# Local attention and a gated product on one core: scores in four 64x64 tiles, and another order of the stays

## The chip, the core and the metric

The kernel runs on one core of a Trainium2 chip. The metric is device time of one execution in microseconds (us). Three runs of the kernel before gave 747.78 us in the median (745.87 to 752.30).

The engines that matter here: TensorE (PE in the profile) multiplies; its weight loads are listed apart (PEld). VectorE (DVE) and ScalarE (ACT) do the element-wise work, SyncE (SP) issues the transfers. GpSimd (POOL) is all but unused.

## The reference

```python
def _attn_ref(q, k, v, n_global, n_local):      # 4 batches, 8 heads, 768 tokens, 64 wide
    scores = (1 / np.sqrt(D)) * np.matmul(q, k.transpose(0, 1, 3, 2))
    rel = pos[:, None] - pos[None, :]
    is_global = pos[None, :] < n_global           # 8
    is_local = (rel >= 0) & (rel < n_local)       # 96
    ...                                           # bias -slope[head] * distance
    scores = np.where(is_global | is_local, scores + bias, -1e9)
    a = softmax(scores)
    return np.matmul(a, v)

def _moe_ref(x, w_a, w_b, w_out):               # 3072 x 512, 512 x 1536, 1536 x 512
    a = x @ w_a
    b = x @ w_b
    return a * b @ w_out
```

A token sees at most 96 tokens behind it and the first 8 of its sequence. The attention's output, 3072 tokens by 512, is x of the gated product. Weights come as 64-bit floats and are turned into 32-bit ones on the chip.

## The kernel before, in words

**Units and chunk pairs.** The 3072 tokens are six units of 512. The hidden width of 1536 is twelve chunks of 128, taken two at a time as six chunk pairs. Each unit has to meet each chunk pair once: 36 meetings. A *stay* is a stretch in which the weights of a few chunk pairs stay on the core; a *pass* is one unit within a stay. Before, a stay has two chunk pairs. ORDER (line 48) lists pairs 0 and 1 with units 0, 1, 2; pairs 2 and 3 with units 2, 1, 0; pairs 4 and 5 with all six; pairs 2 and 3 with units 5, 4, 3; pairs 0 and 1 with units 3, 4, 5. Where a unit leaves its accumulators and comes back, its partial sums are written out and read again (evict, line 1020).

**A meeting.** Values are split into a high and a low part (split, line 397: a cast and a subtraction), and a product takes three matmuls, high by high, high by low, low by high. In a *plain* meeting (project_plain, line 892) four groups of twelve matmuls, 512 tokens wide, make al and ga for two chunks; VectorE multiplies them (h), and cut (line 919) splits h into hh and hl. In a *Winograd* meeting (project, line 930) seven groups of twelve matmuls, 256 wide, do the same work, with more element-wise work: sums of weight pieces, of token pieces (forms, line 776) and of results. Before, the six meetings of the first stay are plain and thirty are Winograd. Both end with back (line 993), 24 matmuls of 512 columns into four accumulators acc.

**Weights.** to32 (line 329) loads a piece of 512 KB as words (wr) and makes 32-bit floats of it with two ACT and four DVE instructions. Six pieces make a chunk pair. In the first stay the pieces are split at once into the tiles w (convert_plain); for later use, convert makes the Winograd sums and writes them to DRAM (dw), and load_w reads them back and splits them. Chunk pairs 0 and 1 are thus converted twice, 48 pieces in all.

**Attention.** A granule is one unit by one pair of heads: 24 granules, four blocks of 128 tokens each. For a block (line 561), two matmuls of 128 by 128 by 168 columns make the scores of 64 tokens of both heads each: q is laid out with zeros so that one head's 64 channels meet its own keys alone, and rows of the result are 64 tokens of head 0, then of head 1. These go to one bank, ps. DVE adds the mask and takes the minimum (line 579), ACT makes exp and the sum (line 595), DVE or ACT normalizes. For unit 0 the probabilities are turned on TensorE (direct, line 695, tile pt); for the others on DVE and through DRAM (turn, carry; tiles tt, mir, px, py). values (line 662) multiplies with v, in tiles of 64 columns, two side by side, one for each head, into pa. Units 0, 1, 2 leave their result on the core in X; units 3, 4, 5 go to DRAM (dx) and are loaded back. Splitting X gives xp (plain) or xf (Winograd).

**Order.** Every operation is put on a list with a due time, its reads and writes, and the cost that the planner assumes (Schedule, line 134). order() runs a clock of its own over it and gives every engine its operations in a fixed sequence; where ACT or DVE can do a copy, it picks one. Tables of numbers (START, SPANS, CONV, ...) set the due times: SPANS is the stretch of passes in which a unit's attention is done, CONV that in which a chunk pair is converted. On the chip each engine keeps its sequence and waits where an input is late.

## Time and profile before

| what | us |
|---|---|
| median of three runs | 747.78 |
| profiled execution, device time | 750.77 |
| its span, first to last instruction | 748.9 |
| PE busy | 705.6 |
| PEld busy | 632.9 |
| DVE busy | 580.1 |
| ACT busy | 390.3 |
| end of the first pass (last back of unit 0 with pair 1) | 112.5 |
| end of the first stay | 231 |
| last matmul ends | 743.15 |

The page of the profile gives busy time by engine, then the span in 40 equal slices with a digit of tenths for each engine, the clock that TensorE was granted and what the transfers moved. Groups of instructions are listed by line with their mean duration and the idle time ahead of them. Timeline rows give start and duration of single instructions or runs of them. A row's duration holds a tail in which the next instruction is already running, so what an instruction occupies is read from start to start. A matmul of two 32-bit operands shows as two records; the counts in the timeline are records.

### The profile page before, as it was taken

How to read it: one execution, taken by the hardware profiler on the slowest of the kernel's cores; microseconds unless marked ns; L12 is line 12 of the kernel's file. 1: busy time of each engine (PE TensorE's matmuls, PEld its weight loads, DVE VectorE, ACT ScalarE, POOL GpSimd, SP SyncE). 2: the span in 40 equal slices, each digit the busy share in tenths (PEclk: the TensorE clock that was granted, in tenths of full speed). 3: DMA queues.
4: the chain of work that ended last, by engine and by line, in shares of the span. 5: the costliest groups of instructions: out<-in, count | busy, mean ns of one | idle time of the engine just before them, and what ended most of it. 6: DMA issues, size and time to landing. Idle time of an engine off the chain costs nothing.

```text
span 748.9 us, 13720 instructions
## 1 busy us (share of the span) xinstructions
PE 705.6 (94%) x4888; PEld 632.9 (85%) x4888; DVE 580.1 (77%) x1601; ACT 390.3 (52%) x980; POOL 1.8 (0%) x8
## 2 busy tenths in 40 slices
PE   4889798998989999999999999999999999999996
PEld 4767677776789889989999888999999999999995
DVE  5899989787789879988999798957467475676643
ACT  2897577456547676557665554633434332342310
POOL 0000000000000000000000000000000000000000
PEclk8999899998999999999999999999999999999999
DMA  7578898999988989998879798542423234232411
GB/s 287 195 245 274 277 301 300 286 331 285 289 323 255 322 305 314 325 320 287 281 268 317 245 288 252 207 155 85 141 71 103 81 113 133 92 112 101 127 71 60
DMA packets 71868, 165.25 MB, mean 221 GB/s; under 512 B 8304, under 2 KB 26864, under 8 KB 70000
## 3 DMA queue, kind: packets, MB, share of 16 engines
q1 hardware_dynamic: 71792, 164.30, 65.8%
q8 instruction: 40, 0.66, 0.4%
q14 instruction: 36, 0.29, 0.1%
HBM read 113.41 MB, written 50.86 MB: 219 GB/s over the span
## 4 chain that ended last, share of the span: by engine, by line
PE 50%; DVE 21%; DMA 19%; ACT 6%; issue 2%; SPq 1%; DVEq 0%; ACTq 0%
PE acc L1003 16%; PE al L861 15%; PE ga L861 11%; DMA wr<-wts 9%; PE ps L564 3%; DVE tt L654 2%; DMA qk<-qk 2%; PE pa L668 2%; DVE t L579 2%; DMA py<-mir 2%; ACT t L595 2%; DVE wm L389 2%; DVE wm L372 2%; DMA wl_A<-dw_A 2%; PE ga L880 1%
## 5 line engine op out<-in xcount | busy, mean ns | idle before, releaser
L1003 PE MATMUL acc<-w_O,hh 128*128 128x512 f32 x576 | 196.4, 400 | 0.7 <-DVE w_O L320 0.7
L1003 PEld LDWEIGHTS acc<-w_O,hh 128*128 128x128 f32 x576 | 108.3, 188 | 23.8 <-DVE w_O L320 1.5
L1003 PE MATMUL acc<-w_O,hl 128*128 128x512 f32 x288 | 113.5, 394 | 0.0
L595 ACT ACTIVATE t<-t,sm 128x168 f32<-128x168 f32 x192 | 81.9, 428 | 39.4 <-DVE sm L579 39.0
L861 PE MATMUL al<-xf_T,w_S 128*128 128x256 f32 x720 | 97.5, 285 | 3.8 <-ACT s L310 3.8
L564 PE MATMUL ps<-qk 128*128 128x168 f32 x384 | 79.2, 338 | 20.6 <-DVE sm L579 13.7
L861 PEld LDWEIGHTS al<-xf_T,w_S 128*128 128x128 f32 x720 | 91.7, 190 | 5.8 <-ACT s L310 4.4
L564 PEld LDWEIGHTS ps<-qk 128*128 128x128 f32 x384 | 63.7, 207 | 31.0 <-DVE sm L579 19.5
L310 ACT COPY s<-al 128x512 f32<-128x512 f32 x70 | 40.9, 584 | 83.6 <-PE al L861 77.7
L579 DVE CUSTOM_DVE_ANT_0 t<-ps,mask 128x168 f32<-128x168 f32 x192 | 56.5, 323 | 17.9 <-PE ps L564 17.7
L310 ACT CAST hh<-h 128x512 fp32r<-128x512 f32 x62 | 38.2, 618 | 58.1 <-DVE h L320 33.5
L1003 PEld LDWEIGHTS acc<-w_O,hl 128*128 128x128 f32 x288 | 54.2, 188 | 9.5
L945 DVE TENSOR_TENSOR s<-ga,s 128x512 f32<-128x512 f32 x60 | 41.0, 683 | 21.9 <-PE ga L861 21.2
L320 DVE TENSOR_TENSOR hl<-h,hh 128x512 fp32r<-128x512 f32 x72 | 48.6, 683 | 8.9 <-ACT hh L310 8.6
L861 PE MATMUL ga<-xf_T,w_S 128*128 128x256 f32 x360 | 49.2, 286 | 1.2 <-DVE s L945 1.2
L861 PEld LDWEIGHTS al<-xf_B,w_A 128*128 128x128 f32 x360 | 46.7, 189 | 2.5 <-issue 0.3
L861 PE MATMUL al<-xf_B,w_A 128*128 128x256 f32 x360 | 48.5, 284 | 0.0
L861 PE MATMUL al<-xf_T,w_A 128*128 128x256 f32 x360 | 48.3, 284 | 0.0
L861 PE MATMUL ga<-xf_B,w_A 128*128 128x256 f32 x360 | 48.2, 284 | 0.0
L861 PE MATMUL ga<-xf_B,w_S 128*128 128x256 f32 x360 | 48.2, 283 | 0.0
L861 PEld LDWEIGHTS ga<-xf_T,w_S 128*128 128x128 f32 x360 | 45.8, 190 | 1.9 <-DVE s L945 1.6
L654 DVE STREAM_TRANSPOSE tt<-t 128x256 f32<-128x256 f32 (+1 forms) x160 | 45.9, 344 | 0.7 <-ACT t L632 0.5
(99 smaller groups left out, 1179.6 us busy)
## 6 DMA issues: line engine op xcount, KB each, us to landing
wr<-wts SPq DMA_DIRECT2D x48, 512.0 KB, 4.6
qk<-qk SPq DMA_DIRECT2D x24, 976.0 KB, 8.8
mir<-tt SPq DMA_DIRECT2D x20, 768.0 KB, 4.1
vt<-vd SPq DMA_DIRECT2D x24, 512.0 KB, 5.7
X<-dx SPq DMA_DIRECT2D x11, 1024.0 KB
part<-o SPq DMA_DIRECT2D x32, 256.0 KB, 3.6
px<-mir SPq DMA_DIRECT2D x60, 128.0 KB, 3.8
wl_S<-dw_S SPq DMA_DIRECT2D x28, 256.0 KB, 3.0
```

Source lines behind the costliest of these rows:

```text
L310: self.nc.scalar.copy(out(), src())
L320: lambda e: self.nc.vector.tensor_tensor(out(), a(), b(), op=op),
L372: lambda e: nc.vector.scalar_tensor_tensor(mi(), high(), -0x40000000, mi(), op0=ALU.bitwise_and, op1=ALU.bitwise_or),
L389: lambda e: nc.vector.tensor_tensor(mi(), mi(), low(), op=ALU.add),
L564: nc.tensor.matmul(ps[:, s * KW : s * KW + KW], qk[:, (2 * i + s) * P : (2 * i + s) * P + P], qk[:, k0 : k0 + KW], start=True, stop=True, ...
L579: lambda e, i=i, w=w, ps=ps, j=j, kind=kind: nc.vector.tensor_tensor_reduce(t[:, i, w], ps[:, w], self.mask[p][:, kind, w], -0.125, 3.0e38 ...
L595: lambda e, i=i, w=w, j=j: nc.scalar.activation(t[:, i, w], t[:, i, w], AF.Exp, bias=sm[:, 0, j : j + 1], scale=-1.0, accum_out=sm[:, 1, j ...
L654: nc.vector.transpose(dst[:, s, b, e0 : e0 + n], src)
L668: nc.tensor.matmul(pa[64 * h : 64 * h + 64, i * P : i * P + P], vt[:lanes, v0 : v0 + 64], k[:, 2 * h : 2 * h + 2, :, i].rearrange("p g s k ...
L861: self.nc.tensor.matmul(bank[:, ab * HT : ab * HT + HT], w[:, a, (2 * ab + c) * P : (2 * ab + c) * P + P], x[:, b, c], start=first, stop=F ...
L945: lambda e: nc.vector.tensor_tensor(s[:, :], bank[:, :], s[:, :], op=ALU.add),
L1003: self.nc.tensor.matmul(acc[i][:, :], a[:, rows], w[:, b], start=first and f == 0 and k == 0, stop=False, skip_group_check=True,)
```

## The change

**Scores.** For two blocks at a time, q is laid out without zeros, and each head's scores are matmuls of 64 rows by 64 columns: head h reads partitions 64h to 64h+63, the two halves of 64 tokens go to columns 0 to 63 and 64 to 127, and the heads write to two different banks. A half of tokens takes 168 columns in one matmul or in two (104 and 64): six matmuls a block and twelve for two blocks, where there were two a block. q with keys shrinks from 1952 to 1440 columns, the masks' table from 1344 to 672, and a result row is a token, so a mask tile is made head by head (eight mask instructions instead of four, half as wide). The table is loaded ahead of the first q and keys.

**Stays.** The first stay has chunk pairs 0, 1, 2, all plain, and units 0 to 3: twelve plain meetings, 24 Winograd. Then stays of pairs 3 and 4 (units 3, 2, 1, 0), pair 5 (0, 1, 2, 3), pairs 5 and 2 (4, 5), 3 and 4 (5, 4), 0 and 1 (4, 5): 18 passes instead of 15. A pair that stays is not loaded again. Pairs 0, 1 and 2 are converted twice now, 54 pieces. Unit 3 leaves its result on the core too. For units 1, 2, 3 the value product of a granule is put on the list after the scores of the next.

**Unit 0 in halves.** Its first two granules hold tokens 0 to 255 of all eight heads, the other two tokens 256 to 511 (entry). Its split, its products and its cut are done by halves of 256 tokens, the first half's before the second half's attention is done. Due times of the start are tables of their own now.

```diff
@@ constants @@
-ORDER = ((0, (0, 1, 2)), (1, (2, 1, 0)), (2, (0, 1, 2, 3, 4, 5)), (1, (5, 4, 3)), (0, (3, 4, 5)))
-PASSES = [(g, u) for g, us in ORDER for u in us]
-SPANS = {1: (0.0, 0.5), 2: (0.5, 1.5), 3: (2.5, 5.0), 4: (5.0, 7.5), 5: (7.5, 10.0)}
-NEAR = (0, 1, 2)
-STD = tuple((0, u) for u in NEAR)
+STAYS = (
+    ((0, 1, 2), (0, 1, 2, 3), True),
+    ((3, 4), (3, 2, 1, 0), False),
+    ((5,), (0, 1, 2, 3), False),
+    ((5, 2), (4, 5), False),
+    ((3, 4), (5, 4), False),
+    ((0, 1), (4, 5), False),
+)
+PASSES = [(k, u) for k, stay in enumerate(STAYS) for u in stay[1]]
+SPANS = {1: (0.0, 0.6), 2: (0.85, 1.6), 3: (1.6, 2.6), 4: (3, 7), 5: (6.79, 11.5)}
+NEAR = (0, 1, 2, 3)
...
-START = 44000.0
+START = 25980.0
...
+HALF0 = 24080.0
+HALF1 = 35730.0
...
+def entry(u, g, i):
+    if u:
+        return g, i
+    return 2 * (g % 2) + i // 2, 2 * (g // 2) + i % 2
@@ granule_ops @@
+        for r in range(2):
             self.count += 1
-            tag = "psS" if u else FIRST["psS"][self.count % len(FIRST["psS"])]
-            ps = self.bank(tag, f"ps{n}_{i}")
-
-            def scores(e, i=i, ps=ps):
-                for s in range(2):
-                    k0 = QN + i * KB + 64 * s
-                    nc.tensor.matmul(
-                        ps[:, s * KW : s * KW + KW],
-                        qk[:, (2 * i + s) * P : (2 * i + s) * P + P],
-                        qk[:, k0 : k0 + KW],
-                        start=True,
-                        stop=True,
-                        skip_group_check=True,
+            tags = self.early_bank("psS", u, p, self.count)
+            ps = [self.bank(tags[h], f"ps{n}_{r}_{h}") for h in range(2)]
+
+            def scores(e, r=r, ps=ps):
+                for b in range(2):
+                    i = 2 * r + b
+                    q0, k0, c0 = i * P, QN + i * KB, b * KW
+                    for s, c, k, w in ((1, 0, 64, KW), (0, 0, 64, KX), (0, KX, 0, 64)):
+                        for h in range(2):
+                            rows = slice(64 * h, 64 * h + 64)
+                            nc.tensor.matmul(
+                                ps[h][64 * s : 64 * s + 64, c0 + c : c0 + c + w],
+                                qk[rows, q0 + 64 * s : q0 + 64 * s + 64],
+                                qk[rows, k0 + k : k0 + k + w],
+                                start=True,
+                                stop=True,
+                                skip_group_check=True,
+                                tile_position=(64 * h, 64 * s),
+                            )
+
+            op(due, scores, [qk], ps, pe=720)
-            op(due, scores, [qk], [ps], pe=580)
...
+        if before:
+            before()
...
-            op(due, turn, ts, [(tt, half)], dve=2 * dve(256) + 2 * dve(128))
+            op(due, turn, ts, [(tt, half)], dve=dve(512) + dve(256))
...
@@ values: unit 0 alone @@
+            a, h = 2 * (p % 2), p // 2
+            self.copy(
+                due + VLAG,
+                lambda: x[:, a : a + 2, HT * h : HT * h + HT],
+                lambda: pa[:, :].rearrange("p (a b) -> p a b", a=2),
+                T,
+                [pa],
+                [(x, (a, h)), (x, (a + 1, h))],
+                psum=True,
+            )
...
@@ attention @@
+        late = None
         for p in range(NPAIR):
+            then = self.granule_ops(u, p, dues[p], x, d, late)
+            if u in LAGGED:
+                late = then
+            else:
+                then()
+        if late:
+            late()
...
@@ plain_forms @@
+        for hs, at in ((((0,), due[0]), ((1,), due[1])) if u == 0 else (((0, 1), due),)):
+            c = slice(HT * hs[0], HT * hs[-1] + HT)
+            n = HT * len(hs)
+            for p in range(NPAIR):
+                f = done[p]
...
@@ project_plain @@
+        for hs, at in ((((0,), due[0]), ((1,), due[1])) if i == 0 else (((0, 1), due),)):
+            c = slice(HT * hs[0], HT * hs[-1] + HT)
+            w = HT * len(hs)
+            st = 12 * pe(w)
+            for f in range(2):
+                ws = [self.w[fp, PLAIN[2 * f + k]] for k in range(2)]
+                al, ga = self.bank("al", f"al{n}_{f}{hs}"), self.bank("ga", f"ga{n}_{f}{hs}")
+                s = self.sbuf([P, T], F32, "s", f"s{n}_{f}{hs}", 3)
+                h = hb[f]
+                t = at + 2 * f * st
+                self.plain_product(t, al, ws, 0, x, hs)
+                self.copy(
+                    t + st,
+                    lambda s=s, c=c: s[:, c],
+                    lambda al=al, c=c: al[:, c],
+                    w,
+                    [al],
+                    [s],
+                    psum=True,
+                )
+                self.plain_product(t + st, ga, ws, 1, x, hs)
...
@@ run @@
-        x0 = self.attention(0, 0.0, START - ATT0)
-        self.convert_plain(0, START - CONV0, STEP0)
+        x0 = self.attention(0, STEPS0)
+        self.convert_plain(0, QUADS0)
+        xf = {0: self.plain_forms(0, (HALF0 - FORM0, HALF1 - FORM0), x0)}
+        self.convert_plain(1, QUADS1)
+        self.convert_plain(2, QUADS2)
-        xf = {0: self.plain_forms(0, START - FORM0, x0)}
-        self.convert_plain(1, START + CONV1, 2500.0)
...
-            if i and PASSES[i - 1][0] != s:
-                for fp in (2 * s, 2 * s + 1):
-                    self.load_w(fp, t - 0.9 * fpt + (fp % 2) * fpt, 0.09 * fpt)
+            if i and PASSES[i - 1][0] != stay:
+                for k, fp in enumerate(fps):
+                    if fp not in STAYS[stay - 1][0]:
+                        self.load_w(fp, t - 0.9 * fpt + k * fpt, 0.09 * fpt)
...
+                if not i:
+                    due = [h + k * GAP for h in (HALF0, HALF1)]
...
+                if not i:
+                    prev([d + 48 * pe(HT) for d in due])
+                    prev = None
...
@@ build @@
-        width = 8 * KW
-        nc.sync.dma_start(tiles["qk0"], a["qk"][0, 0])
+        width = 4 * KW
         nc.sync.dma_start(
             tiles["X"].rearrange("p a b -> p (a b)")[:, :width], a["pos"][:, :width]
         )
         nc.sync.dma_start(tiles["slope"], a["pos"][:, width:])
+        nc.sync.dma_start(tiles["qk0"], a["qk"][0, 0])
```

What this does to the sequences is shown at two places. First TensorE, around the first product of unit 0; ps is a bank of scores, pa a value product, al and ga the products with chunk pair 0, w0_ its weights. Before:

```order
L564 MATMUL ps1_0_3_578<-qk0_78 128x168 x2
L880 MATMUL al0_0_0_593<-xp0_0_313,w0_A11_0_499 128x512 x3
L880 MATMUL al0_0_0_593<-xp0_1_448,w0_A11_0_499 128x512 x3
L880 MATMUL al0_0_0_593<-xp0_2_565,w0_A12_0_539 128x512 x3
L880 MATMUL al0_0_0_593<-xp0_3_581,w0_A12_0_539 128x512 x3
L880 MATMUL ga0_0_0_620<-xp0_0_313,w0_A11_0_499 128x512 x3
L880 MATMUL ga0_0_0_620<-xp0_1_448,w0_A11_0_499 128x512 x3
```

After, in unit 0's last granule (ps0_3; L581 is the score line, L943 the product line; the product of the first chunk stands 28 rows further up):

```order
L581 MATMUL ps0_3_1_0_574<-qk1_79 64x168
L581 MATMUL ps0_3_1_1_576<-qk1_79 64x168
L581 MATMUL ps0_3_1_0_574<-qk1_79 64x104
L581 MATMUL ps0_3_1_1_576<-qk1_79 64x104
L581 MATMUL ps0_3_1_0_574<-qk1_79 64x64
L581 MATMUL ps0_3_1_1_576<-qk1_79 64x64
L943 MATMUL al0_0_1(0,)_591<-xp0_0_361,w0_A21_0_423 128x256 x3
L943 MATMUL al0_0_1(0,)_591<-xp0_1_372,w0_A21_0_423 128x256 x3
L943 MATMUL al0_0_1(0,)_591<-xp0_2_458,w0_A22_0_456 128x256 x3
L943 MATMUL al0_0_1(0,)_591<-xp0_3_482,w0_A22_0_456 128x256 x3
```

Before, the first product stands behind all four granules of unit 0, and a product row is 512 wide. Now products of the first half, 256 wide, stand among the scores of unit 0's last granule (ps0_3), and a block's scores are six rows in two banks.

Second VectorE, where unit 1's token tiles xp1 are made, which the second pass waits for; wm is a weight piece on its way, hl the low half of a product. Before:

```order
L389 ISA wm1_5_1061<-wr1_5_1012,wm1_5_1061 128x1024
L579 ISA t2_0_1140,sm2_0_1141<-ps2_0_0_1127,mask1_135 128x168
L579 ISA sm2_0_1141 128x1
L579 ISA t2_0_1140,sm2_0_1141<-ps2_0_0_1127,mask1_135 128x168
L579 ISA sm2_0_1141 128x1
L909 TENSOR_TENSOR h0_1_1_1149<-ga0_1_1_1065,s0_1_1_1063 128x512
L320 TENSOR_TENSOR w1_O1_0_1143<-wm1_5_1061,w1_O1_0_1143 128x512
L320 TENSOR_TENSOR xp1_0_1110<-X_81,xp1_0_1110 128x512
```

After:

```order
L988 TENSOR_TENSOR h0_2_0_1432<-ga0_2_0(1,)_1569,s0_2_0(1,)_1519 128x256
L342 TENSOR_TENSOR w2_O1_0_1592<-wm2_5_1510,w2_O1_0_1592 128x512
L342 TENSOR_TENSOR hl0_2_0_1459<-h0_2_0_1432,hh0_2_0_1450 128x256
L988 TENSOR_TENSOR h0_2_1_1564<-ga0_2_1(1,)_1602,s0_2_1(1,)_1558 128x256
L334 CAST xp1_1_1628<-X_81 128x512
L334 CAST hh0_2_1_1567<-h0_2_1_1564 128x256
L376 TENSOR_SCALAR wm3_0_1619<-wm3_0_1619 128x512
L342 TENSOR_TENSOR hl0_2_1_1590<-h0_2_1_1564,hh0_2_1_1567 128x256
L342 TENSOR_TENSOR xp1_0_1626<-X_81,xp1_0_1626 128x512
L342 TENSOR_TENSOR xp1_1_1628<-X_81,xp1_1_1628 128x512
```

Before, xp1 stands behind the last piece of chunk pair 1 (w1_O1); now behind the last piece of chunk pair 2 (w2_O1), and behind the third meeting of unit 0 (h0_2, hl0_2). VectorE's instructions up to the last hl of the first pass are 359 before and 390 now.

490 lines of the change are left out of this document (255 added, 235 removed).

## The prediction

> **What bounds the kernel now.** I read the page first, then stretches of the span, then the waits, then the cadence of single matmuls.
>
> The page: span, busy time, and in 40 slices PE's busy tenths and the transfers' GB/s.
>
> ```profile
> span 748.9 us, 13720 instructions
> PE 705.6 (94%) x4888; PEld 632.9 (85%) x4888; DVE 580.1 (77%) x1601; ACT 390.3 (52%) x980; POOL 1.8 (0%) x8
> PE   4889798998989999999999999999999999999996
> GB/s 287 195 245 274 277 301 300 286 331 285 289 323 255 322 305 314 325 320 287 281 268 317 245 288 252 207 155 85 141 71 103 81 113 133 92 112 101 127 71 60
> ```
>
> PE is busy 94%, and what it misses lies in the first third. The same in stretches that end where passes end (busy us of PE, PEld, DVE, ACT, POOL; then clock, transfer share, GB/s):
>
> ```profile
> 0.00:50.00 50.00, 33.02 (x272) 29.10 (x273) 36.98 (x170) 33.21 (x123) 1.75 (x8) 0.93 0.66 234
> 50.00:112.50 62.50, 56.25 (x306) 44.21 (x305) 57.75 (x205) 44.65 (x129) 0.00 (x0) 0.92 0.89 287
> 112.50:231.00 118.50, 109.18 (x648) 91.19 (x648) 95.98 (x298) 69.66 (x179) 0.00 (x0) 0.94 0.89 297
> 231.00:309.00 78.00, 76.55 (x578) 70.18 (x578) 70.75 (x202) 52.82 (x133) 0.00 (x0) 1.00 0.92 307
> 309.00:468.00 159.00, 155.49 (x1189) 142.82 (x1188) 141.31 (x397) 90.19 (x236) 0.00 (x0) 1.00 0.86 286
> 468.00:743.20 275.20, 275.15 (x1905) 255.39 (x1903) 176.61 (x336) 99.81 (x187) 0.00 (x0) 1.00 0.33 109
> ```
>
> From 468 us on PE never stops. Between 50 and 112.5 DVE is busy 57.75 of 62.50; from 50 to 309 the transfers are at 0.89 to 0.92. PE's waits by releaser (total, times, longest) put DVE first:
>
> ```profile
> PE ps L564 <- DVE sm L579: 13.7, 11, 4.0
> ```
>
> Now what PE's work takes at its best pace: three pieces of the chain, then single records, where a step is read from start to start.
>
> ```profile
> 143.87 2.79 PE ga L880 x12
> 606.86 5.60 PE acc L1003 x24
> 612.46 1.44 PE al L861 x12
> ```
>
> ```profile
> 20.20 0.27 PE L707 MATMUL pt<-ident,t 128*64 128x128 f32 x1
> 20.31 0.27 PE L704 MATMUL pt<-ident,t 128*104 128x128 f32 x1
> ...
> 24.11 0.44 PE L668 MATMUL pa<-px,vt 104*64 104x128 f32 x4
> 24.39 0.39 PE L668 MATMUL pa<-py,vt 128*64 128x128 f32 x4
> 24.61 0.39 PE L668 MATMUL pa<-px,vt 104*64 104x128 f32 x4
> ...
> 25.71 0.39 PE L668 MATMUL pa<-py,vt 128*64 128x128 f32 x4
> 26.03 0.32 PE L704 MATMUL pt<-ident,t 128*104 128x128 f32 x1
> ...
> 65.04 0.84 PE L564 MATMUL ps<-qk 128*128 128x168 f32 x4
> 65.60 0.51 PE L1003 MATMUL acc<-w_O,hh 128*128 128x512 f32 x1
> ...
> 112.14 0.40 PE L1003 MATMUL acc<-w_O,hh 128*128 128x512 f32 x1
> ...
> 742.75 0.40 PE L1003 MATMUL acc<-w_O,hh 128*128 128x512 f32 x1
> ```
>
> A Winograd meeting is 7 x 1.44 + 5.60 = 15.68, a plain one 4 x 2.79 + 5.60 = 16.76. A block's scores take 0.56 (65.04 to 65.60), so one matmul of 168 columns 0.28. A value product takes 1.92 (24.11 to 26.03), a turn 0.11. Before: 30 x 15.68 + 6 x 16.76 + 96 x 0.56 + 24 x 1.92 + 64 x 0.11 = 470.4 + 100.6 + 53.8 + 46.1 + 7.0 = 677.9. The last matmul ends at 743.15, so 65.3 us are lost to idle time and a low clock. Counting PE's sequence up to the ends of passes in the same way gives 74.2 of work by 112.5 (36 blocks, 7 value products, 64 turns, 96 matmuls of plain products, 48 of back; 38 lost), 174.0 by 231 (57 lost), 249.2 by 309 (60 lost), 402.1 by 468 (66 lost), and nothing after. So the time is PE's work, plus what the start loses while DVE and the transfers cannot feed PE, plus 5.75 behind the last matmul.
>
> **PE's work after the change.** Plain meetings: six more, 6 x (16.76 - 15.68) = +6.5. Unit 0's three meetings in halves: 288 matmuls at 1.44/12 = 0.120 instead of 144 at 2.79/12 = 0.2325, +1.1. Turns and value products keep their counts.
>
> Scores: two blocks were four matmuls, 1.12. Now they are twelve, and each of the four 64x64 tiles streams 168 columns for each block. If all four tiles run side by side, two blocks stream 2 x 0.28 = 0.56. To this comes the change of tile shape. The value product shows it: its groups step by 0.22, but the first takes 0.28 and the way out, 25.71 to 26.03, takes 0.32; in and out 0.16. I take 0.72 for two blocks: 48 x (0.72 - 1.12) = -19.2. The value rows also show that two column tiles do run side by side: four records, two matmuls of 128 columns, step by 0.22, and one matmul of 168 columns takes 0.28, so 128 of them would take 0.21 alone. Two row tiles at once no row shows. From above: at the value product's step of 55 ns a record, 24 records and the 0.16 make 1.48, dearer than now by 0.36, or 17 us in all. From below: if the switches hide under neighbours, 0.56, 8 us better than my figure.
>
> The Trainium skill speaks against this edit in one place: "TensorEngine Tiling (Array Packing)", Key Properties, says that a change of tiling mode drains TensorE. By that rule 48 more score groups pay a drain each; the trace agrees, with the 0.16 in and out of the value product, and without it the sum would be 48 x 0.16 = 7.7 us lower.
>
> Sum: 677.9 - 19.2 + 6.5 + 1.1 = 666.3.
>
> **What the start loses.** VectorE sets the end of the first pass, since unit 1 needs it and so does the last cut. Its costs:
>
> ```profile
> L320 DVE TENSOR_TENSOR h<-s 128x256 f32<-128x256 f32 x90 | 37.2, 418 | 1.1
> L389 DVE CUSTOM_DVE_ANT_0 wm<-wr,wm 128x1024 uint16<-128x1024 uint16 x48 | 32.8, 683 | 1.2 <-ACT wr L382 0.5
> L372 DVE SCALAR_TENSOR_TENSOR wm<-wr,wm 128x512 int32<-128x512 int32 x48 | 32.8, 683 | 0.3
> L362 DVE TENSOR_SCALAR wm<-wm 128x512 int32<-128x512 int32 x48 | 20.0, 418 | 0.4
> L320 DVE TENSOR_TENSOR w_A<-wm,w_A 128x512 fp32r<-128x512 f32 x10 | 6.8, 681 | 0.1
> ```
>
> The six pieces of chunk pair 2 come into the first pass: each 2 x 0.418 + 2 x 0.683 + 0.681 = 2.88, together 17.3. The products and low halves of unit 0 are 24 of 256 (0.418) where they were 8 of 512 (0.683): +4.6. Four score tiles fewer and fewer, wider turns and copies give back some 3. That is 19 us of durations in 31 more instructions (359 to 390); each duration holds a tail under the next one, as here 0.57 against a step of 0.48:
>
> ```profile
> 8.47 0.57 DVE L495 TENSOR_SCALAR X<-X,nf 128x672 f32<-128x672 f32 x1 [3.72 <-DMA X<-pos]
> 8.95 0.56 DVE L496 TENSOR_SCALAR X<-X,nf 128x672 f32<-128x672 f32 x1
> ```
>
> So +16 of occupied time. Against it: these rows wait 3.72 for the table, which now goes first and is half as long; I take 3 off. The first pass then ends at 112.5 + 16 - 3 = 125.5, if DVE stays as full as it was (94.7 busy of 112.5). PE's work up to there, counted from the new sequence, is 83.4: 32 blocks, 7 value products, 64 turns, 288 half-wide matmuls, 72 of back. Loss 42, against 38. Ends: if half of DVE's 17.8 us of idle time goes, because PE's products start early and hand it work, the loss is 33; if DVE is only as full as from 112.5 to 231 (0.81), its 111 us end at 137 and the loss is 54.
>
> Passes 2 to 4 have three meetings each, so PE has 196 us of work there. The transfers listed up to there, added up by tile size, are some 54 MB, 275 GB/s. From 112.5 to 231 before, 297 GB/s ran beside 100 us of PE work, that is, transfers held PE back; it lost 18.5. I charge 6.
>
> Over the whole program transfers fall a little:
>
> ```profile
> wr<-wts SPq DMA_DIRECT2D x48, 512.0 KB, 4.6
> qk<-qk SPq DMA_DIRECT2D x24, 976.0 KB, 8.8
> wl_S<-dw_S SPq DMA_DIRECT2D x28, 256.0 KB, 3.0
> ```
>
> q with keys: 24 x (976 - 720) KB less, six raw pieces and six weight loads more, one unit load less: 3 MB less in all. But passes 9 to 12 (pair 5 alone) have 71 us of PE work, and 25 MB are listed in them: 350 GB/s, where the best slice above has 331. Charged for passes 5 to 12: 8; before, 309 to 468 lost 6.5. For the rest, no loss, as now.
>
> **Sum.** 666.3 + 42 + 6 + 8 = 722.3, with 5.75 a span of 728. The profiled execution took 750.77 for a span of 748.9, so 730; it lay 3 above the median of the runs. I predict 727 us. With the ends above: best, 0.56 a score group and 33 lost at first, 710; worst within this account, 54 lost at first and ten more in passes 9 to 12, 749.
>
> **Rivals.**
>
> *The row tiles take turns.* If the two heads' tiles cannot stream together, the sequence, which puts the heads next to each other, leaves nothing side by side: a block streams 2 x (168 + 104 + 64) columns, at 0.28 for 168 that is 1.12, two blocks with the switch 2.40. 48 x (2.40 - 0.72) = +81, some 15 of it under DVE's time at the start: 793. It decides from 1.2 a group on. For it: no row shows two row tiles. Against it: two column tiles do overlap, and each head has its own bank. The Trainium skill, "TensorE: Matmul & The Clock Gate", Measured speedup vs the span model, measured row and column tiles together, 10.6 times for sixteen; by that rule this rival falls, but no row here can show it. 7%.
>
> *Issue paces the small matmuls.* Twelve small matmuls with their loads replace four; at 1.1 to 1.48 a group (the bound from above) it is 745 to 763. Against it: the value product's 55 ns is two overlapped matmuls of 0.21 each in four records, which its columns explain without issue. 11%.
>
> *VectorE stretches the first pass.* Chunk pair 2's pieces stand ahead of xp1 on DVE, so a late piece holds unit 1 and all PE behind it; the loss is 54 and not 42: 739. For it: DVE 0.92 busy from 50 to 112.5. 8%.
>
> *The short stay runs dry.* 25 MB at 300 GB/s are 83 us for 71 of work, some 10 more than charged: 737. For it: shares near 0.9 up to 468 us. 12%.
>
> *The halves fill the start.* Loss of 30 or less in the first pass and little behind it: under 714. For it: PE idles or runs slow for 38 of 112.5, and most of unit 0's work no longer waits for its last granule. 17%.
>
> My own case, 714 to 738, has 45%.
>
> **Chances.** A difference of over 1% (under 740.3, over 755.3) is about what a measurement tells from none. Faster: 45 + 17, 10 of the short stay's 12, 4 of the first pass's 8, 1 of issue's 11: 0.77. Within 1%: 2 + 4 + 6 = 0.12. Slower: 4 + 7 = 0.11. The range 704 to 750 leaves out the row tiles' 7, the upper part of the issue case (6) and some 5 below.
>
> **What would show it.** Score groups of two blocks that step by about 0.72 from start to start, heads' records starting a few tens of ns apart; 2.4 would be the first rival, 1.1 to 1.5 the second. The first unit-0 product before 35 us, the first pass ending near 125; 137 and later would be the third rival. PE's idle time in the passes of pair 5 near 5; over 12 would be the short stay. From about 480 us on, PE without a gap. I am wrong at the root if the score groups cost less and the end doesn't follow: then PE's work was not what the first 300 us wait for.

## The result, and the profile after

Over four runs of each the changed kernel takes 725.02 us in the median (720.99 to 728.68) and the kernel before 748.65 us (745.87 to 752.30); the ratio is 0.968, with a 95% interval of 0.9613 to 0.9748. The forecast was 727. The profiled execution of the changed kernel is the slowest of its four, 728.68 us for a span of 726.4; the profile of before had 750.77 and 748.9. So it is 22.5 us of span that have to be found.

The page of the changed kernel: span, busy time by engine, PE's busy tenths and GB/s in 40 slices.

```profile
span 726.4 us, 15134 instructions
PE 693.5 (95%) x5584; PEld 605.8 (83%) x5584; DVE 578.9 (80%) x1544; ACT 387.7 (53%) x989; POOL 1.8 (0%) x8
PE   5698998999999999999999999999999999999996
GB/s 296 213 163 259 269 294 300 267 305 250 304 280 303 253 335 247 262 266 228 221 249 232 294 259 301 245 201 230 233 337 151 146 59 102 131 145 102 74 73 62
```

Stretches of the changed kernel that end where passes end (length; busy time of PE, PEld, DVE, ACT, POOL; then clock, transfer share, GB/s). The second row ends with the first pass, the third with the second, the fifth with the first stay, the seventh with pair 5's passes.

```profile
0.00:50.00 50.00, 33.49 (x397) 28.75 (x398) 44.43 (x185) 38.57 (x130) 1.83 (x8) 0.90 0.65 233
50.00:118.70 68.70, 64.44 (x638) 56.39 (x638) 63.67 (x211) 50.16 (x144) 0.00 (x0) 0.98 0.83 261
118.70:208.50 89.80, 85.94 (x714) 66.98 (x714) 67.28 (x231) 50.59 (x150) 0.00 (x0) 0.98 0.84 284
208.50:272.80 64.30, 64.30 (x489) 50.83 (x488) 50.67 (x142) 41.67 (x117) 0.00 (x0) 1.00 0.92 301
272.80:328.60 55.80, 55.72 (x367) 46.14 (x366) 42.81 (x97) 29.31 (x65) 0.00 (x0) 1.00 0.75 257
328.60:473.40 144.80, 143.23 (x1235) 129.56 (x1233) 130.57 (x333) 80.65 (x199) 0.00 (x0) 1.00 0.77 255
473.40:545.60 72.20, 71.85 (x570) 65.80 (x569) 68.48 (x150) 37.32 (x84) 0.00 (x0) 1.00 0.73 247
545.60:720.10 174.50, 174.50 (x1188) 161.35 (x1186) 110.25 (x202) 59.46 (x105) 0.00 (x0) 1.00 0.33 103
```

Subtract PE's busy time from the length of each row: PE idles 26.6 us in these eight rows, and 37.6 in the six rows of before. Multiply each length by what its clock lacks of 1.00: before, 50 x 0.07 + 62.5 x 0.08 + 118.5 x 0.06 = 15.6 us; now 50 x 0.10 + 68.7 x 0.02 + 89.8 x 0.02 = 8.2. That is an upper bound of what a slow clock cost, since PE idles for part of those stretches. So of the 22.5 us, 10.9 are idle time, up to 7.4 are clock, and the remaining 4 or so are PE's own work and the tail behind the last matmul (5.75 before, 6.3 now).

PE's waits of the changed kernel by releaser (total, times, longest): the wait for DVE that came first before, 13.7 us, has shrunk to 1.9.

```profile
PE ps L581 <- DMA qk<-qk: 7.0, 1, 7.0
PE pt L749 <- DVE t L661: 4.2, 2, 3.5
...
PE ps L581 <- DVE sm L602: 1.9, 3, 1.3
```

Single records of PE in the changed kernel: start, duration, shape, records. First the first product of unit 0, then two score groups between plain products of unit 1.

```profile
35.22 2.86 PE L943 MATMUL al_0(0,)_510<-xp,w_A 128*128 128x256 f32 x12
...
128.53 0.82 PE L581 MATMUL ps<-qk 64*64 64x168 f32 x24
129.28 3.05 PE L943 MATMUL ga_0(0, 1)_1772<-xp,w_A 128*128 128x512 f32 x12
132.26 0.82 PE L581 MATMUL ps<-qk 64*64 64x168 f32 x24
133.00 3.06 PE L943 MATMUL al_1(0, 1)_1823<-xp,w_A 128*128 128x512 f32 x12
136.00 0.82 PE L581 MATMUL ps<-qk 64*64 64x168 f32 x24
```

The first product starts at 35.22 where it started at 50.01. A score group steps by 0.75 (128.53 to 129.28). But a product between two groups steps by 2.98 (129.28 to 132.26), where a product alone takes 2.79: a whole turn, group and product, takes 3.72 to 3.74, so a group costs 0.94 and not 0.72. In this trace a product with a group on one side only takes 2.89, so each edge of a group costs its neighbour about 0.1. Over the 36 groups that stand without a wait between products or back's matmuls, a group with both edges costs 0.94 in the median (0.91 to 1.05).

With the prediction's own paces (a group at 0.72), PE's sequence up to the ends of passes gives this account. What a group costs beyond 0.72 stands under "lost" here, and so does time at a low clock:

| up to the end of | ends at | PE's work | lost | lost by the forecast |
|---|---|---|---|---|
| the first pass | 118.7 | 83.4 | 35.3 | 42 |
| the fourth pass | 328.6 | 279.8 | 48.8 | 48 |
| pair 5's passes | 545.6 | 491.0 | 54.6 | 56 |
| the last matmul | 720.1 | 666.2 | 53.9 | 56 |

### The profile page after: what moved, and what is told of

Same layout as the page of the kernel before. It is cut to its first block, busy times and chain, and to the rows that moved or that the text cites. A ratio compares the mean times of both kernels' runs of the same rounds, so it can differ in the third digit from the quotient of the medians.

```text
span 726.4 us, 15134 instructions
## 1 busy us (share of the span) xinstructions
PE 693.5 (95%) x5584; PEld 605.8 (83%) x5584; DVE 578.9 (80%) x1544; ACT 387.7 (53%) x989; POOL 1.8 (0%) x8
## 4 chain that ended last, share of the span: by engine, by line
PE 68%; DMA 12%; DVE 11%; ACT 5%; issue 2%; SPq 1%; DVEq 0%; ACTq 0%
PE acc L1099 19%; PE al L922 16%; PE ga L922 12%; DMA wr<-wts 8%; PE ps L581 4%; PE pa L701 3%; ACT t L619 1%; DMA py<-mir 1%; DVE tt L677 1%; DMA X<-dx 1%; DVE t L602 1%; DVE wm L394 1%; ACT wm L369 1%; DVE wm L411 1%; SPq L323 1%
## 5 line engine op out<-in xcount | busy, mean ns | idle before, releaser
L922 PE MATMUL al<-xf_T,w_S 128*128 128x256 f32 x576 | 76.8, 283 | 0.0
L922 PEld LDWEIGHTS al<-xf_T,w_S 128*128 128x128 f32 x576 | 72.2, 189 | 0.5
L332 ACT CAST hh<-h 128x512 fp32r<-128x512 f32 (+1 forms) x62 | 36.6, 592 | 50.2 <-DVE h L342 22.5
L1099 PEld LDWEIGHTS acc<-w_O,hl 128*128 128x128 f32 x288 | 54.3, 188 | 10.5 <-DVE hl L342 1.1
L581 PEld LDWEIGHTS ps<-qk 64*64 64x64 f32 x1152 | 36.3, 142 | 28.1 <-issue 14.2
L581 PE MATMUL ps<-qk 64*64 64x168 f32 (+2 forms) x1152 | 43.6, 278 | 14.4 <-DMA qk<-qk 7.0
L369 ACT ACTIVATE wm<-wr 128x512 f32<-128x512 f32 x54 | 36.2, 670 | 34.7 <-DMA wr<-wts 25.2
L342 DVE TENSOR_TENSOR hl<-h,hh 128x512 fp32r<-128x512 f32 (+1 forms) x78 | 49.8, 642 | 5.2 <-ACT hh L332 4.9
L677 DVE STREAM_TRANSPOSE tt<-t 128x512 f32<-128x512 f32 x80 | 41.1, 552 | 0.8 <-ACT t L658 0.4
L404 ACT ACTIVATE wr<-wr 128x512 int32<-128x512 uint32 x54 | 36.2, 673 | 7.2 <-DMA wr<-wts 4.3
L701 PE MATMUL pa<-px,vt 104*64 104x128 f32 x384 | 38.9, 278 | 1.2 <-DMA px<-mir 1.2
L701 PE MATMUL pa<-py,vt 128*64 128x128 f32 x384 | 38.0, 273 | 1.1 <-DMA py<-mir 1.0
```

The lines of the kernel that those rows point to most:

```text
L332: self.nc.scalar.copy(out(), src())
L342: lambda e: self.nc.vector.tensor_tensor(out(), a(), b(), op=op),
L369: lambda e: nc.scalar.activation(m(), high().bitcast(F32), AF.Abs),
L404: lambda e: nc.scalar.activation(low(), low().bitcast(U32), AF.Copy, scale=2.0**-29),
L581: nc.tensor.matmul(ps[h][64 * s : 64 * s + 64, c0 + c : c0 + c + w], qk[rows, q0 + 64 * s : q0 + 64 * s + 64], qk[rows, k0 + k : k0 + k + ...
L677: nc.vector.transpose(dst[:, :, e0 : e0 + n], src[:, :, c0 : c0 + 32 * n].rearrange("p j (e k) -> p j e k", e=n),)
```

## The experiments

Each starts from the changed kernel. "First pass" ends are those of its profiled execution.

### What a score group costs

**Each group twice.** All matmuls of a group are issued a second time into the same place.

```diff
-                for b in range(2):
+                for b in (0, 1, 0, 1):
                     i = 2 * r + b
```

> The new kernel with each group's twelve score matmuls issued twice into the same places (the same result). Theory (PE's work is what the end waits for): 0.56 more a group without another change of tile shape, 48 x 0.56 = 27, of which some 5 hide at the start: 745 to 752. Rival (up to 300 us the scores hide behind VectorE and the transfers): 36 of 48 groups lie there, 7 to 12 more, 732 to 737.

Measured: 751.88 us (748.30 to 756.84), ratio to the kernel before 1.0064 [1.0029, 1.0098], so 27 us over the changed kernel. Its timeline, two groups of twice the records:

```profile
128.79 3.04 PE L943 MATMUL al_0(0, 1)_1930<-xp,w_A 128*128 128x512 f32 x12
131.76 1.41 PE L581 MATMUL ps<-qk 64*64 64x168 f32 x48
133.10 3.06 PE L943 MATMUL ga_0(0, 1)_1988<-xp,w_A 128*128 128x512 f32 x12
```

The group steps by 1.34 in place of 0.75, so 24 records, the work alone, take 0.59 (48 x 0.59 = 28 us, and 27 were measured). By the forecast's 0.28 for 168 columns, two tiles at a time would take 1.12 for them and four at once 0.56: four tiles do run side by side. The product beside the group takes 2.97 as before. So of a group's 0.94, 0.59 is work and 0.35 is the way in and out: 0.16 inside the group's step and 0.19 in the two neighbours. Nearly all time that is added to PE comes out at the end, so PE is what the kernel waits for over most of the span. In the first pass it is so only in part: there 16 groups add 9.4 us, and its end moves by 4.6, to 123.3.

**The heads one after the other.** The loop over the heads goes outside, so a head's six matmuls of two blocks follow each other.

```diff
-                for b in range(2):
...
-                    for s, c, k, w in ((1, 0, 64, KW), (0, 0, 64, KX), (0, KX, 0, 64)):
-                        for h in range(2):
+                for h in range(2):
+                    for b in range(2):
...
+                        for s, c, k, w in ((1, 0, 64, KW), (0, 0, 64, KX), (0, KX, 0, 64)):
```

> The new kernel with the twelve score matmuls of a group in another sequence: all six of head 0, then all six of head 1, so that neighbours differ in their column tile but not in their row tile. Theory (all four tiles run side by side): with one head at a time a group streams 2 x 0.56, steps by about 1.25 to 1.45 instead of 0.75, and 48 groups cost 24 to 33 more, some 5 of it hidden at the start: 744 to 753. Rival (row tiles take turns anyway, only column tiles overlap): the group keeps its step within 0.1, 724 to 729.

Measured: 738.20 us (737.45 to 740.29), ratio 0.9896 [0.9844, 0.9948], 13 us over the changed kernel: about half of what the theory asked for and more than the rival allowed. The timeline of this kernel:

```profile
132.49 1.16 PE L581 MATMUL ps<-qk 64*64 64x168 f32 x24
133.58 3.05 PE L943 MATMUL ga_0(0, 1)_1772<-xp,w_A 128*128 128x512 f32 x12
```

The group steps by 1.09 in place of 0.75, 0.34 more, and 48 x 0.34 = 16. The same matmuls in another order take 0.34 longer, so with the heads in turn more of them runs at once. Had the heads run quite apart, the work of 0.59 would have doubled; it costs 0.34 more, so some overlap is left. Whether the streams of the two heads or their weight loads overlap less in this order, the run does not show.

### What sets the end of the first pass

**VectorE's work on chunk pair 2.** The forecast put the end of the first pass down to VectorE, with chunk pair 2's pieces on top. Here the four DVE operations of each of that pair's six pieces are not issued in its first conversion (dv drops the instruction, for this one and the three like it); the weights of that pair are therefore unfinished numbers.

```diff
-            lambda e: nc.vector.tensor_tensor(mi(), mi(), low(), op=ALU.add),
+            dv(lambda e: nc.vector.tensor_tensor(mi(), mi(), low(), op=ALU.add)),
```

> The new kernel without VectorE's four instructions (clamp, shift, merge, add) in the first conversion of chunk pair 2, so that this conversion is left unfinished and its weights have other values in the first stay; loads, ScalarE's part, the split and the sequence of all other instructions stay. Theory (VectorE's work sets the end of the first pass): 24 instructions of 13 us less, 11 occupied, so the first pass ends at 108 to 111 instead of 118.7, and the whole at 714 to 718. Rival (ScalarE, the transfers or PE itself set it): it ends within 3 of 118.7, 722 to 727.

Measured: 726.66 us (725.53 to 728.39), ratio 0.9667 [0.9601, 0.9734]. The first pass ends at 118.9, 0.2 later than in the changed kernel. The theory falls.

**PE's work on pairs 1 and 2.** If not VectorE, then PE?

```diff
-            for p in range(NPAIR):
+            for p in span:
                 w = ws[p // 2]
...
+                span = range(2 if i == 0 and fp else NPAIR)
```

> The changed kernel with half of the steps of each gate and up product left out where the first unit meets pairs 1 and 2 (96 matmuls of 0.12 us, 11.5 us of TensorE between 60 and 115 us). Theory: from 60 us on the first pass is set by TensorE's own work; the pass ends 9 to 12 us earlier, at 107 to 110, and the total is 713 to 717 us. Rival: the loads and conversions of the weight pieces set the end of the first pass, and TensorE only fills the time; it ends at 116 to 119 as it was and the total is 722 to 727 us.

Measured: 727.78 us (721.94 to 732.22), ratio 0.9697 [0.9607, 0.9787]. The first pass ends at 116.7, 2.0 earlier with 11.5 us less of work, and the total is that of the rival. This theory falls as well. The two together are the finding. The stretch from 80 to 119 us, first the changed kernel, then pair 2's conversion light, then less PE work, one fence each (busy time of PE, PEld, DVE, ACT, POOL; clock, transfer share, GB/s):

```profile
80.00:119.00 39.00, 38.20 (x379) 33.06 (x378) 35.91 (x115) 27.56 (x73) 0.00 (x0) 1.00 0.90 280
```

```profile
80.00:119.00 39.00, 37.61 (x372) 32.54 (x366) 24.64 (x89) 27.31 (x73) 0.00 (x0) 1.00 0.89 283
```

```profile
80.00:119.00 39.00, 32.20 (x307) 26.77 (x305) 35.88 (x114) 26.97 (x73) 0.00 (x0) 0.96 0.91 272
```

PE is busy 98% and DVE 92% of this stretch. With DVE relieved of 11 us, PE stays full (37.61); with PE relieved, DVE stays full (35.88). Two engines have about as much to do as the stretch is long, and taking work from one leaves the other. That these two hold the end together is the likely reading and not shown: no run relieves both at once. Each end of a pass is that of one execution, so a difference of 2 us is not read as an effect.

**VectorE's work on chunk pair 0**, the same edit for the pair that the first product needs.

> The changed kernel with VectorE's four operations of each piece of chunk pair 0's first conversion left out (24 operations, about 13 us of VectorE; the weights of that pair have other values). Between 10 and 50 us VectorE is busy 98% and ScalarE 93%, so theory: VectorE sets how early the first product comes and how dense TensorE is up to 50 us; the first product comes at 29 to 32 us in place of 35, the first pass ends at 110 to 114 in place of 119, and the total is 716 to 720 us. Rival: ScalarE or the order of the work sets the start just as much; first product within 2 us of 35, total 723 to 727 us.

Measured: 723.05 us (720.70 to 725.12), ratio 0.9647 [0.9575, 0.9719]. The first product starts at 35.09, the first pass ends at 117.5: the rival, if barely in the total. The stretch from 10 to 40 us, of the changed kernel and then of this run:

```profile
10.00:40.00 30.00, 21.88 (x247) 18.37 (x248) 29.47 (x128) 28.61 (x102) 0.00 (x0) 0.83 0.62 227
```

```profile
10.00:40.00 30.00, 21.25 (x282) 17.50 (x276) 20.99 (x112) 29.18 (x105) 0.00 (x0) 0.89 0.71 248
```

DVE falls from 29.47 to 20.99 of 30 us, and ACT stays at 29. At the start ACT is as full as DVE; whether ACT or the order of the work holds the start then, no run separates.

**The table loaded late.** The mask's table goes behind the first q and keys, as it did before.

```diff
+        nc.sync.dma_start(tiles["qk0"], a["qk"][0, 0])
...
         nc.sync.dma_start(tiles["slope"], a["pos"][:, width:])
-        nc.sync.dma_start(tiles["qk0"], a["qk"][0, 0])
```

> The new kernel with the masks' table loaded behind the first q and keys, as before. Theory: VectorE's first mask step, at 5.75 now, comes at 7 to 8.5; the first scores are read 1 to 2 later, the first pass ends 1 to 3 later, in all 725 to 728. Rival: the first mask step moves but the first pass keeps its end within 1, because the first exponentials wait for q and keys, which now land earlier than 7.0: 723 to 726.

Measured: 726.02 us (724.68 to 728.81), ratio 0.9658 [0.9591, 0.9724]; the first pass ends at 119.1. DVE's first mask step starts at 6.90 where it started at 5.75, and the first pass ends 0.4 later: as the rival has it, nothing comes of the delay there, while the total does not tell theory and rival apart.

**Unit 0 whole.** Its split, products and cut are done for 512 tokens at once again, the second half's due time standing for both.

```diff
-        for hs, at in ((((0,), due[0]), ((1,), due[1])) if u == 0 else (((0, 1), due),)):
+        for hs, at in ((((0, 1), due),)):
```

> The new kernel with unit 0's split, products and cut over all 512 tokens at the second half's due time; granules, stays and scores unchanged. Theory (the halves let PE and VectorE start on products early): the first product comes at 45 to 50 instead of 35.2, the first pass ends 6 to 9 later than 118.7, in all 731 to 734. Rival (VectorE's 108 us of work set the end of the first pass either way): it ends within 2 of 118.7, in all 723 to 727, since 1.1 us of PE work goes too.

Measured: 736.11 us (734.53 to 741.89), ratio 0.9876 [0.9800, 0.9951], 11 us over the changed kernel. The first pass ends at 124.3, 5.6 later, although PE's work in it is 1.1 us less. The first product starts only at 59.72, later than the 45 to 50 that were expected and than the 50.01 of the kernel before: its due time is the second half's, and so this run may take more from the start than the halves alone. Its first 50 us and the rest of its first pass:

```profile
0.00:50.00 50.00, 31.13 (x348) 24.40 (x348) 42.75 (x173) 38.83 (x131) 1.83 (x8) 0.83 0.67 233
50.00:124.30 74.30, 70.79 (x540) 55.58 (x540) 66.71 (x202) 52.78 (x139) 0.00 (x0) 0.95 0.79 244
```

Against the changed kernel's rows, the clock is 0.83 and 0.95 for 0.90 and 0.98, worth up to 50 x 0.07 + 74.3 x 0.03 = 5.7. So about half of the 11 us lies in the first pass, and the clock can be most of that. Of the rest some 5 us go in the fourth pass of this run (272.8 to 328.6 in the changed kernel, 260.9 to 336.2 here, with 14.5 us more of PE's work in it); why there is open.

**Fewer bytes.** Transfers are the third resource that is nearly full. In this run the two buffers of the raw pieces are fixed tiles, so that the half that is not loaded holds older numbers.

```diff
-            lambda e: nc.sync.dma_start(raw[:, :].bitcast(I64), self.a["wts"][fp, piece]),
+            lambda e: nc.sync.dma_start(
+                raw[:, : 2 * CN // (2 if fp else 1)].bitcast(I64),
+                self.a["wts"][fp, piece][:, : CN // (2 if fp else 1)],
+            ),
```

> The changed kernel with only half the bytes of each weight piece of chunk pairs 1 to 5 brought in for the first conversion (30 pieces of 512 KB, so 7.9 MB less; the other half of a piece keeps older numbers, so the weights have other values), in the same order of TensorE's work. Between 60 and 118 us the transfers are busy 73 to 96% of the time at 276 GB/s, and neither less work on VectorE nor less work on TensorE moved the end of the first pass. Theory: the transfers set it, since they go through one queue in order and the pieces make the others wait; 12 pieces less 256 KB are 3.1 MB or 11 us at 276 GB/s, the first pass ends at 107 to 113 us in place of 119, the passes of units 1 and 2 gain some more, and the total is 707 to 717 us. Rival: no single resource sets it, since the order of the small steps over all engines does; the first pass ends at 116 to 119 us and the total is 720 to 727 us.

Measured: 720.19 us (719.94 to 720.64), ratio 0.9613 [0.9552, 0.9674]. Total and first pass (it ends at 117.2) are the rival's, so transfers do not set it alone either: no single one of the resources that were relieved does. The second pass and the third, in this run:

```profile
117.20:201.10 83.90, 83.64 (x713) 65.71 (x714) 67.56 (x232) 49.93 (x148) 0.00 (x0) 1.00 0.85 270
201.10:265.40 64.30, 64.30 (x489) 50.82 (x488) 50.50 (x141) 41.12 (x117) 0.00 (x0) 1.00 0.87 279
```

The second pass takes 83.9 us in place of 89.8, and its clock never falls. I do not count this as shown for the transfers: in the profiled executions of the two runs with a lighter VectorE, where the bytes are as in the changed kernel, the second pass takes 84.7 and 85.7, and in the ones with the late table and with less PE work 89.0 and 89.3. With fewer bytes the four runs lie within 0.7 us of each other, where the changed kernel's spread over 7.7; that speaks for the transfers as what tips the pass one way or the other, and it is no proof.

### The stays

**Old stays; and old stays with unit 0 whole.** Two runs put back the stays of before, the first with the halves (and the start tables of the change), the second without (and with the start tables of before). SPANS, CONV and NEAR are those of before too, and chunk pair 2 has no plain conversion.

```diff
-    ((0, 1, 2), (0, 1, 2, 3), True),
-    ((3, 4), (3, 2, 1, 0), False),
...
+    ((0, 1), (0, 1, 2), True),
+    ((2, 3), (2, 1, 0), False),
+    ((4, 5), (0, 1, 2, 3, 4, 5), False),
+    ((2, 3), (5, 4, 3), False),
+    ((0, 1), (3, 4, 5), False),
```

> The new kernel with the stays, spans and conversion times of before, unit 0 still in halves. Theory: the new stays cost 6.5 us of PE work and pay with less loss in passes 2 to 4 (12 lost there, where before lost 20), so without them 725 to 731, about even. Rival 1: the new stays are the main gain, 735 or more. Rival 2: they are a pure cost of PE work, 718 to 720. In the trace: the first pass with two chunk pairs ends near 100 instead of 118.7, and the stretch up to 231 has transfers near 0.9 and a granted clock under 0.96 again.

> The new kernel with the stays of before (two chunk pairs each, units 0 to 2 first, its tables of due times) and unit 0 whole; the four-tile scores, the smaller q and table and the table first in the queue stay. Theory (PE's work is what the end waits for nearly everywhere): a group of two blocks steps by 0.75 plus some 0.15 of drain ahead of it where two blocks took 1.2, so 48 groups save 14 to 16 us, and the start some 3: about 730. Rival (the scores of the first passes hide behind VectorE and the transfers, and 56 of 96 blocks lie in the first stay): only 6 to 8 us come through, about 740.

Measured: 764.93 us (763.51 to 767.41), ratio 1.0261 [1.0208, 1.0314], and 764.61 (762.09 to 766.71), 1.0246 [1.0188, 1.0305]. The first meets its rival 1 (735 or more), but far above that bound; the second lies far above theory and rival. The undoing was not clean: the kernel before puts six of chunk pair 2's forms straight into tiles that are free from the start, and these two runs had the tile places of the changed kernel. So both were repeated with the places of before; chunk pair 2's first six forms are split at once again, and not loaded for the second stay.

```diff
+        elif fp < 2:
+            k = OWN[name] + (3 if OWN[name] > 11 else 6) * fp
         else:
-            k = PLACE[fp] + (FORMS + ("O0", "O1")).index(name)
+            k = ((12 if fp % 2 == 0 else 3) + (FORMS + ("O0", "O1")).index(name)) % 18
```

> The changed kernel with the stays of the kernel before (pairs 0 and 1 plain under units 0 to 2, then 2 and 3, 4 and 5, 2 and 3, 0 and 1), and this time also with that kernel's tiles: six of chunk pair 2's forms go straight into tiles that are free from the start, and the rest and pair 3 into those that the plain pairs leave. Theory: the +40 us of old_stays came from the tiles that it took and not from the stays, so this run lands near the changed kernel: the stays took 6.5 us more of plain work and saved 27 - 19 = 8 us of loss behind the first pass, so 725 to 738 us, with no pass that loses over 12 us beyond the first. Rival: the old stays do not go together with the new scores and the halves, whatever the tiles; then 755 to 768 us as before.

> The new scores alone: the stays, the tiles and the start tables of the kernel before, the first unit whole. Theory: the scores are worth about 16 us of TensorE's work (0.89 us a group with what it costs its neighbours, against 1.22 for two blocks), so 748 - 16 = 732 us, range 727 to 738. Rival: the new scores need the other parts of the change, because their masks and the two banks a group crowd the first pass; then 745 us or more.

Measured: 759.34 us (756.83 to 764.84), ratio 1.0134 [1.0049, 1.0220], and 760.44 (757.74 to 763.76), 1.0128 [1.0056, 1.0200]. The tiles are worth some 5 us by the medians (9 by the ratios to the kernel before); the rivals were right. With the old stays nothing can be told of the halves, 1 us where they were worth 11. These kernels still differ from the one before, beside the scores, in unit 0's granules by token halves, in the value products of units 1 and 2 that stand behind the next scores, in a bank that the value product shares with one head's scores, and in the planner's price of a transfer.

So with the old stays the kernel with the new scores is slower than the one before, though a group is cheaper. Where the time goes: PE's longest waits of this last run between 105 and 242 us, its second and third pass, and then two of the waits in its timeline; 166.17 is the last score group ahead of the second.

```profile
PE pa L710 <- DMA px<-mir: 21.9, 4, 10.3
PE pa L710 <- DMA py<-mir: 2.3, 4, 1.5
```

```profile
119.82 0.69 PE L710 MATMUL pa<-px,vt 104*64 104x128 f32 x4 [10.33 <-DMA px<-mir]
...
166.17 0.82 PE L590 MATMUL ps<-qk 64*64 64x168 f32 x24
...
184.25 0.69 PE L710 MATMUL pa<-px,vt 104*64 104x128 f32 x4 [6.08 <-DMA px<-mir]
```

PE waits for turned probabilities that come back from DRAM, 24.2 us in two passes. The kernel before waited 3.3 us there, in the same window, and the changed kernel 2.2 over its whole span; first the waits of before with the same place in its timeline, then the groups in the page of the changed kernel:

```profile
PE pa L668 <- DMA px<-mir: 1.8, 1, 1.8
PE pa L668 <- DMA py<-mir: 1.5, 4, 0.6
```

```profile
153.21 0.73 PE L564 MATMUL ps<-qk 128*128 128x168 f32 x4
...
171.40 0.69 PE L668 MATMUL pa<-px,vt 104*64 104x128 f32 x4 [1.76 <-DMA px<-mir]
```

```profile
L701 PE MATMUL pa<-px,vt 104*64 104x128 f32 x384 | 38.9, 278 | 1.2 <-DMA px<-mir 1.2
L701 PE MATMUL pa<-py,vt 128*64 128x128 f32 x384 | 38.0, 273 | 1.1 <-DMA py<-mir 1.0
```

The probabilities do not come back later than before. From the last score group of a unit's last granule to its first value product, unit 2 takes 18.1 us in that run (166.17 to 184.25), 18.2 in the kernel before (153.21 to 171.40) and 20.9 in the changed one (166.34 to 187.25). What differs is what PE has to do meanwhile: it is busy for 7.5 us of that stretch here, for 15.4 in the kernel before and for 19.4 in the changed one. The longest wait is of the same kind: unit 1's 19.0 us (100.87 to 119.82) hold 7.0 of work. So the sequence of TensorE leaves a hole there, with too little work between the scores and the value product; which of the differences made the planner order it so, no run shows.

And the clock: that run's first pass, its second and third, and its twelfth, in which unit 5 comes in,

```profile
0.00:105.60 105.60, 84.45 (x784) 65.09 (x784) 87.63 (x332) 72.80 (x231) 1.83 (x8) 0.87 0.70 227
105.60:242.10 136.50, 112.04 (x887) 90.75 (x887) 108.30 (x314) 79.28 (x211) 0.00 (x0) 0.90 0.88 291
...
527.90:578.50 50.60, 44.37 (x302) 41.96 (x303) 31.89 (x56) 22.24 (x40) 0.00 (x0) 0.90 0.42 131
```

lose up to 105.6 x 0.13 + 136.5 x 0.10 + 50.6 x 0.10 = 32 us to it, twice the 15.6 of before, and PE idles 52 us in these three rows, where all six rows of before have 37.6. What PE saved on scores went into waits and the low clock beside them. The changed kernel's stays are thus worth some 34 us beside the other parts (759.34 - 725.02), of which the forecast's account of stays, +6.5 of plain work against a smaller loss behind the first pass, holds only a small part. No run has the new stays with the old scores, so what the stays are worth by themselves is open.

## Why the prediction was right

**The total.** 727 was forecast, 725.02 measured; for the profiled execution 730 and 728.68. That it came so near is luck. With a group at 0.94, PE's work is 666.2 + 48 x 0.22 = 676.8 us and the loss 720.1 - 676.8 = 43.3, where the forecast had 666.3 and 56: one 10.5 too low, the other 12.7 too high, and nothing ties the two. The frame held: the time is PE's work plus what is lost ahead of pair 5's end, and behind that PE never stops (174.50 of 174.50).

**The scores, -19.2: mis-sized.** "I take 0.72 for two blocks". The step is 0.75, but 0.19 more lies in the neighbours, so 0.94. The old block, counted in the same way around one product in the profile before, costs 0.58 (60.03 to 63.40 less 2.79), and between back's matmuls 0.66 (65.04 to 67.10 less six at 0.2333):

```profile
60.03 0.73 PE L564 MATMUL ps<-qk 128*128 128x168 f32 x4
60.49 3.07 PE L880 MATMUL ga<-xp,w_A 128*128 128x512 f32 x12
63.40 0.40 PE L1003 MATMUL acc<-w_O,hh 128*128 128x512 f32 x1
...
67.10 0.73 PE L564 MATMUL ps<-qk 128*128 128x168 f32 x4
```

Over the 35 old blocks that stand without a wait it is 0.56 in the median, as the forecast took it. So the edit saves 1.12 - 0.94 = 0.18 a group, some 9 us and not 19. The balance of the span gives much the same: PE's busy time less what the clock cost fell by 690.0 - 685.3 = 4.7 (705.6 - 15.6 and 693.5 - 8.2), and with the 7.6 us that the plain meetings and halves add, the scores gave some 12. The work itself was forecast well, 0.56 against 0.59. It is the 0.16 for the way in and out that was too small: it was read from value products that lie beside turns and other value products, and 0.35 is what it takes between products. That TensorE drains where the tiling mode changes is what the Trainium skill says in "TensorEngine Tiling (Array Packing)", Key Properties; these runs agree, at 0.35 us a group or 17 us in all.

**The first pass, 42: 35.3 measured, and the reason fell.** "VectorE sets the end of the first pass". The sum put 16 us of DVE's work on top of its old idle time; it fitted in, for DVE's idle time in the pass went from 17.8 us to 10.6, PE's products having come 15 us earlier. The lower end that the forecast named for that case, 33, is near. Taking DVE's work out again moves the end by 0.2 us: PE stays busy for 96% from 80 us on in that run, and with pair 0 relieved ACT stays busy for 97% from 10 to 40. That these hold the end is likely and not shown. Of the 3 us for the table at most 0.4 are there.

**Passes 2 to 4, 6: 13.5 measured** (48.8 - 35.3), 10 of it in the second pass. Part is the dearer group, 20 groups at 0.22; of the rest, about 4 us idle and up to 1.8 of clock are in this execution, some 3 stay open, and three of the runs above show the second pass 4 to 6 us shorter.

**Passes 5 to 12, 8: 5.8 measured**, and nothing lost behind, as forecast.

**The rivals.** *The row tiles take turns* (2.4 a group): 0.75 measured, and the heads' order matters. The rule that was quoted against it, from "TensorE: Matmul & The Clock Gate" in the Trainium skill, Measured speedup vs the span model, holds here: row and column tiles ran together, at 0.59 us for the work of a group. *Issue paces*: 24 records in 0.59 are 25 ns a record, so the 55 ns of the value product were not the pace of issue. *VectorE stretches the first pass* to 137: 118.7. *The short stay runs dry*: PE idles 0.35 us in pair 5's 72.2 us, and transfers run at 247 GB/s there and not at 350, so 17.8 MB moved there (247 x 72.2) and not the 25 that are listed. *The halves fill the start*: the first pass lost 35.3 and not 30, and under 714 it did not get, though putting unit 0 whole again costs 11 us. "PE's work was not what the first 300 us wait for" would have made the forecast wrong at the root. Of the double scores' 28 us 27 came out, so over the whole it is; in the first pass it is not so alone, where 11.5 us less moved the end by 2.0 and 9.4 more by 4.6; and the old stays say that it holds only as long as the order keeps PE in work while its operands come.

The text ahead of the prediction says 18 passes instead of 15; counted again, the kernel before has 18 as well (3, 3, 6, 3 and 3). No term rests on it.

**What the forecast had no term of its own for** is the clock: its losses hold idle time and low clock together, and up to 7.4 of the 22.5 us are clock. Nor did it see that the parts need each other: it put the stays down as 6.5 us of work against a few of loss, and without them the other parts are slower than the kernel before.

## What to carry to other kernels

Price a small-tile group by the whole turn, from one neighbour's start to the next neighbour's start, and not by its own step: more than a third of it was in the change of tile shape, and half of that in the neighbours. Where two engines are each over 90% busy in a stretch, taking work from one need not move its end, and a sum that lets one of them set the end is not confirmed by a total that comes out right. Where an engine waits for a result, measure first how long that result took: here it took as long as before, and the work that used to cover it was gone. A part of a change that saves work can cost time without the other parts, so each part's worth holds only beside the others.

## What the runs showed of the hardware

**The clock falls without a full pause.** The clock goes to half in stretches of 3.4 us or multiples. In the changed kernel one of them covers 59.2 to 62.6 us. The rows ahead of it:

```profile
55.10 0.49 PE L581 MATMUL ps<-qk 64*64 64x168 f32 x2
56.47 0.81 PE L581 MATMUL ps<-qk 64*64 64x168 f32 x22 [0.87 <-ACT X L332]
58.58 1.39 PE L581 MATMUL ps<-qk 64*64 64x168 f32 x24 [1.30 <-DVE sm L602]
```

No gap is longer than 1.3 us, but in the 3.4 us before 59.2 PE is busy for 0.41 of the time, and the group at 58.58 takes 1.32 to the next start (59.90) where others take 0.75. All fourteen traces here, cut from 10 us on into stretches of 3.4 us that line up with their own falls, show the same. Behind a stretch at full clock in which PE was busy for less than 0.45 the clock fell every time (39 times), behind one with more than 0.65 never, and between the two both are found (18 falls, 30 without). The Trainium skill, "TensorE: Matmul & The Clock Gate", Part 1 on the clock gate, has the half rate come after at least one idle window of about 3.4 us; the window's length agrees, but a window in which PE was busy for 0.41 was enough here, and the measurement decides.

**Four tiles at once.** 24 records of 64 by 64 tiles, up to 168 columns each, take 0.59 us when added to a group, 25 ns a record, and 0.34 us more when the heads are not issued in turn. A product of twelve matmuls of 512 columns takes 2.79 alone, 2.89 with one such group beside it and 2.98 with one on either side.
